# Adding x and three groups' projections on VectorE, and injecting the sums by two 64-column matmuls

## The chip, the cores and the metric

One Trainium2 chip, one core. The metric is the device time of one execution in microseconds. Every kernel was run several times. A run counts as slow when it is over 1.5% above the fastest of its kernel; those are left out of all comparisons. The profile is one traced execution; its span is mostly about 2.1 us shorter than the time, because the time includes start and end. In this kernel TensorE does the matmuls, whose sums gather in PSUM; VectorE and ScalarE do elementwise work and move sums out of PSUM (an eviction). An injection is a matmul with an identity that adds a finished row to the sums in PSUM.

## The reference, cut to what matters

One decode position goes through a cached attention block and an MLP block in parallel, and both are added to the input. Names that begin with `ln` are layer norms.

```python
x  = A_x                                   # (1, 1, 1024)
xn = ln(x)
# A: q = xn @ wq; 4 groups of 8 heads attend to 65536 cached keys each; o @ wo
# B: x1 = xn + shift(gelu(ln(xn) @ w1)) @ w2
#    out_B = x1 + gelu(ln(x1) @ w3) @ w4
out = x + A(xn) + B(xn)
# shift() moves quarters of the features by 1 or 2 positions and fills with zeros;
# with one position nothing is left of them, so its product with w2 is zero
```

The terms `x + xn` are an affine function of `x` (`x * ln_s1 + ln_s2` in the kernel). The output is thus that row, plus the projections of four groups of heads, plus the w4 product.

Of the kernel before, what the change touches and what calls it, by code (L numbers as in the profile page):

```python
# [8 lines left out]
BF16 = mybir.dt.bfloat16  # L9
F32 = mybir.dt.float32  # L10
ACTF = mybir.ActivationFunctionType
ALU = mybir.AluOpType
# [84 lines left out]
def kernel(  # L97
# [14 lines left out]
    nc = tc.nc  # L112
# [3 lines left out]
    D = A_x.shape[-1]  # L116
# [7 lines left out]
    FC = F // P  # L124
# [4 lines left out]
    NU = HKV * NB  # L129
# [3 lines left out]
    const = ctx.enter_context(tc.tile_pool(name="const", bufs=1))  # L133
    small = ctx.enter_context(tc.tile_pool(name="small", bufs=1))
    big = ctx.enter_context(tc.tile_pool(name="big", bufs=SLOTS))
    ppool = ctx.enter_context(tc.tile_pool(name="psb", bufs=1))
# [58 lines left out]
    st = Stream()  # L195

    x_row = ogpool.tile([32, D], BF16, name="x_row", tag="og")
# [4 lines left out]
    ident_f = const.tile([P, P], F32, name="ident_f")  # L202
# [9 lines left out]
    for b in range(2):  # L212
        nc.gpsimd.tensor_copy(
            out=spread[:, 2 * b:2 * b + 2, :].rearrange("p r (a i) -> p r a i", a=4),
            in_=ident_f[:, 64 * b:64 * b + 64].rearrange("p (i r) -> p r i", r=2).unsqueeze(2).to_broadcast([P, 2, 4, 32]))

    qdiag = const.tile([P, LEAD + 4 * P], BF16, name="qdiag")
    nc.gpsimd.memset(qdiag[:], 0.0)
    g_col = const.tile([P, 1], BF16, name="g_col")
    nc.gpsimd.memset(g_col[:], 0.0)  # L220

    psB = ps_B.tile([P, 512], F32, name="psB")

    def row_acc(j, lhsT, rhs, start=False):
        return nc.tensor.matmul(psB[32 * j:32 * j + 32, :], lhsT=lhsT.to_broadcast([lhsT.shape[0], 32]), rhs=rhs, start=start,  # L225
                                stop=False, tile_position=(0, 32 * j), skip_group_check=True)

    x_t = ppool.tile([P, DC, 32], BF16, name="x_t", tag="p")
    for a in range(4):
        nc.vector.transpose(out=x_t[32 * a:32 * a + 32].rearrange("p c j -> p (c j)"),  # L230
                            in_=x_row[:, 256 * a:256 * (a + 1)].rearrange("p (i c) -> p c i", c=DC))
# [3 lines left out]
    def layernorm(src, tag):  # L235
# [39 lines left out]
                          in_=sel8[:].unsqueeze(2).to_broadcast([P, 8, 16]))  # L275

    ln_s1 = const.tile([P, 1], F32, name="ln_s1")
    nc.vector.tensor_scalar(out=ln_s1[:], in0=rstd1[:], scalar1=1.0, scalar2=None, op0=ALU.add)
    ln_s2 = const.tile([P, 1], F32, name="ln_s2")
    nc.vector.tensor_tensor(out=ln_s2[:], in0=negmean1[:], in1=rstd1[:], op=ALU.mult)  # L280
    accx = ppool.tile([1, D], F32, name="accx", tag="p")
    nc.vector.tensor_scalar(out=accx[:], in0=x_row[0:1, :], scalar1=ln_s1[0:1, 0:1], scalar2=ln_s2[0:1, 0:1],
                            op0=ALU.mult, op1=ALU.add)
    for j in range(2):
        row_acc(j, ident_f[0:1, 0:1], accx[0:1, 512 * j:512 * (j + 1)], start=True)

    def row_matmul(acc, rep, cols, widths):
        for c in range(DC):
# [44 lines left out]
    def compute_w12():  # L333
        wt = st.tiles["w12"][:, 0:2 * DC * D].rearrange("p (w c n) -> p w c n", w=2, c=DC)
        ps1 = ps_S.tile([P, SUBS, 512], F32, name="ps1", tag="sc")
        for c in range(DC):
            for q in range(2):
                nc.tensor.matmul(ps1[0:32, q, :], lhsT=xn2_rep[:, c, :], rhs=wt[:, 0, c, 512 * q:512 * (q + 1)],
                                 start=(c == 0), stop=(c == DC - 1), tile_position=(0, 0))
        h1 = ppool.tile([32, 2, 512], BF16, name="h1", tag="p")  # L340
        nc.scalar.activation(out=h1[:], in_=ps1[0:32, 0:2, :], func=ACTF.Gelu_apprx_tanh)
        for c in range(DC):
            for j in range(2):
                row_acc(j, g_col[:], wt[:, 1, c, 512 * j:512 * (j + 1)])
        st.done("w12")

    group = {}
# [42 lines left out]
    def group_weights():  # L390
        nball = group["nball"]
        negmg = small.tile([P, 1], F32, name="negmg")
        nc.vector.tensor_reduce(out=negmg[:], in_=nball[:], axis=AX.X, op=ALU.min)
        wb = small.tile([P, NB], F32, name="wb")
        nc.scalar.activation(out=wb[:], in_=nball[:], func=ACTF.Exp, bias=negmg[:, 0:1], scale=-1.0)
        og = group["og"]
        nc.vector.tensor_scalar(out=og[:], in0=og[:], scalar1=wb[:, 0:1], scalar2=None, op0=ALU.mult)
        lw = small.tile([P, NB], F32, name="lw")
        ol = small.tile([P, DH + 1], F32, name="ol")
        nc.vector.tensor_tensor_reduce(out=lw[:], in0=group["lall"][:], in1=wb[:], scale=1.0, scalar=0.0,  # L400
                                       op0=ALU.mult, op1=ALU.add, accum_out=ol[:, DH:DH + 1])
        return og, wb, ol
# [3 lines left out]
    def compute_v(u):  # L406
        g, b = divmod(u, NB)
        if b == 1:
            og, wb, ol = group_weights()
        vt = st.tiles[("V", u)][:].rearrange("p (s u t d) -> p s u t d", u=SUBS, s=SETS, t=16)  # L410
        oacc = ps_O.tile([P, 512], F32, name="oacc")
        pT = group["p"]
        for e in range(SUBS):
            for t in range(16):
                q = t % 4
                mm = nc.tensor.matmul(oacc[32 * q:32 * (q + 1), :], lhsT=pT[:, e, 32 * t:32 * (t + 1)],  # L416
                                      rhs=vt[:, :, e, t, :], start=(e == 0 and t < 4),
                                      stop=(e == SUBS - 1 and t >= 12), tile_position=(0, 32 * q))
        st.done(("V", u))
        if b == 0:  # L420
            og = ogpool.tile([P, 512], F32, name="og", tag="og")
            nc.scalar.copy(out=og[:], in_=oacc[:])
            group["og"] = og
            return
        nc.vector.scalar_tensor_tensor(out=og[:], in0=oacc[:], scalar=wb[:, 1:2], in1=og[:],  # L425
                                       op0=ALU.mult, op1=ALU.add)
        group_rows(g, og, ol)
        return mm.ins

    oT = {}  # L430
    tail = {}
# [27 lines left out]
        return mm.ins if g == HKV - 1 else None  # L459

    def copy_projection():
        tail["o"] = st.tiles["w4"][0:1, FC * D:FC * D + 2 * D].bitcast(F32)
        nc.vector.tensor_copy(out=tail["o"].rearrange("p (j n) -> p j n", j=2), in_=tail["rows"][0:1, 0:2, :])  # L463

    def add_projection():
        for j in range(2):
            row_acc(j, ident_f[0:1, 0:1], tail["o"][:, 512 * j:512 * (j + 1)])

    def compute_w4(lo, hi):
        wt = st.tiles["w4"]  # L470
# [4 lines left out]
    compute_wq()  # L475
    compute_w3()
    compute_w12()
    for u in range(NU - 1):
        compute_k(u)
# [3 lines left out]
    for g in range(HKV - 1):  # L483
        project(g)
    copy_projection()
    summed = compute_v(NU - 1)
    with tc.issue_after(summed):
        add_projection()
    early = sum(W4_PIECES[:AT_ONCE])
    compute_w4(0, FIRST)  # L490
    with tc.issue_after(tail["gathered"]):
# [2 lines left out]
    with tc.issue_after(projected):  # L494
        compute_w4(early, FC - NARROW)
    sums = ogpool.tile([64, 512], F32, name="sums", tag="og")
    nc.scalar.copy(out=sums[:], in_=psB[0:64, :])
    quarters = [ps_M.tile([P, 512], F32, name="pm_r", tag="pm") for _ in range(2)]

    def quarter_acc(lhsT, rhs, start=False):  # L500
        for h in range(2):
            for j in range(2):
                q = 2 * h + j
                nc.tensor.matmul(quarters[h][32 * q:32 * q + 32, 0:256], lhsT=lhsT(j), rhs=rhs(j, h), start=start, stop=False,  # L504
                                 tile_position=(0, 32 * q), skip_group_check=True)

    def narrow_rows(lo, hi, start=False):
        wt = st.tiles["w4"]
        for c in range(lo, hi):
            quarter_acc(lambda j: hT[:, c:c + 1].to_broadcast([P, 32]),  # L510
                        lambda j, h: wt[:, D * c + 512 * j + 256 * h:D * c + 512 * j + 256 * (h + 1)],
                        start=start and c == lo)

    narrow_rows(FC - NARROW, FC - NARROW + AHEAD, start=True)
    quarter_acc(lambda j: ident_f[0:64, 32 * j:32 * j + 1].to_broadcast([64, 32]),
                lambda j, h: sums[:, 256 * h:256 * (h + 1)])
    narrow_rows(FC - NARROW + AHEAD, FC)

    out_t = ogpool.tile([64, 2, 256], BF16, name="out_t", tag="og")
# [3 lines left out]
                        in_=out_t[31:33].rearrange("p h n -> p (h n)"))  # L523
# [29 lines left out]
```

## The kernel before, the parts the change touches

All weights and the K and V caches pass once through three buffers of 128 x 32768 bf16, in a fixed order. A buffer's next load is issued when the last reader of its present content is done.

```python
stream = ["wq", "w3", "w12", K0, V0, K1, V1, ..., K7, "wo", V7, "w4"]   # each up to 8 MB
W4_PIECES = (8, 12, 5, 2, 1)      # w4's 28 chunks of 256 KB are loaded in five pieces
FIRST, AT_ONCE, NARROW, AHEAD = 3, 1, 8, 5
```

One PSUM tile, `psB`, collects the "first sums": rows 0 to 31 hold output columns 0 to 511, rows 32 to 63 hold columns 512 to 1023 (all 32 rows of a half are equal).

```python
def row_acc(j, lhsT, rhs, start=False):     # one 32-column matmul into half j
    return nc.tensor.matmul(psB[32*j:32*j+32, :], lhsT=lhsT.to_broadcast([lhsT.shape[0], 32]),
                            rhs=rhs, start=start, stop=False, tile_position=(0, 32*j), ...)

# at the start: x * ln_s1 + ln_s2 as one fp32 row, injected through a 1x1 identity
accx = ppool.tile([1, D], F32, name="accx", tag="p")
nc.vector.tensor_scalar(out=accx[:], in0=x_row[0:1, :], scalar1=ln_s1[0:1, 0:1], scalar2=ln_s2[0:1, 0:1], ...)
for j in range(2):
    row_acc(j, ident_f[0:1, 0:1], accx[0:1, 512*j:512*(j+1)], start=True)
...
# near the end: the first three groups' projections, summed in another PSUM tile ("o_acc")
def copy_projection():
    tail["o"] = st.tiles["w4"][0:1, FC*D:FC*D + 2*D].bitcast(F32)       # an unused corner of a buffer
    nc.vector.tensor_copy(out=tail["o"]..., in_=tail["rows"][0:1, 0:2, :])

def add_projection():
    for j in range(2):
        row_acc(j, ident_f[0:1, 0:1], tail["o"][:, 512*j:512*(j+1)])
...
for g in range(HKV - 1): project(g)          # 48 matmuls of one column
copy_projection()
summed = compute_v(NU - 1)                   # last V tile
with tc.issue_after(summed): add_projection()
compute_w4(0, FIRST)                         # w4 chunks 0..2
with tc.issue_after(tail["gathered"]): compute_w4(FIRST, early)    # 3..7
projected = project(HKV - 1)                 # last group, into psB
with tc.issue_after(projected): compute_w4(early, FC - NARROW)     # 8..19
sums = ogpool.tile([64, 512], F32, name="sums", tag="og")
nc.scalar.copy(out=sums[:], in_=psB[0:64, :])
quarters = [...]                             # two PSUM tiles: the output in four quarters of 256
narrow_rows(FC - NARROW, FC - NARROW + AHEAD, start=True)          # chunks 20..24, four matmuls each
quarter_acc(lambda j: ident_f[0:64, 32*j:32*j+1].to_broadcast([64, 32]),
            lambda j, h: sums[:, 256*h:256*(h+1)])                 # inject the first sums
narrow_rows(FC - NARROW + AHEAD, FC)         # chunks 25, 26 (fourth piece), 27 (fifth piece)
# cast the quarters (half on ScalarE, half on VectorE), store
```

## Time and profile before

| | before |
|---|---|
| time, median of the first 3 runs | 400.86 us (400.77 to 400.88) |
| span of the traced execution | 398.7 us |
| TensorE / VectorE / ScalarE busy | 58% / 53% / 7% |
| big DMA queue, share of 16 engines' time | 98.9% |
| loaded | 169.87 MB, 426 GB/s over the span |

The page of the kernel before. The line of busy times gives us, share of the span and the number of instructions of each engine; the queue line gives packets, MB and share of 16 engines' span.

```profile
span 398.7 us, 2595 instructions
...
PE 229.6 (58%) x1372; PEld 44.2 (11%) x878; DVE 209.4 (53%) x155; ACT 27.6 (7%) x36; POOL 5.3 (1%) x28
...
q1 hardware_dynamic: 4128, 169.87, 98.9%
...
HBM read 169.87 MB, written 0.00 MB: 426 GB/s over the span
```

No compute engine is near its limit, and the load queue is. The Trainium skill, "DMA: Bandwidth & Descriptors", section Measured, gives 425 GB/s for a 16 MB transfer that GpSimd issued; the 426 GB/s of this trace, whose loads SyncE issues, agree with it. So the whole of the span is filled with loads at about the rate that one may expect.

The end of the chain of waits of the kernel before (start us, us, what): what ended last, followed back.

```profile
340.47 17.43 DVE big L361 x4
...
357.94 3.64 PE sc L366 x16
...
363.39 33.10 DMA big<-in_B_w_dram
...
396.54 0.34 PE pm_r L504 x4
...
396.90 0.43 DVE out_t L521
```

The last K tile is transposed and multiplied, then its buffer is free, the five pieces of w4 are issued into it, and 33.10 us later the last of them has landed. The pieces are issued behind loads that are still under way, so these 33 us are a place in the stream, not the cost of w4 alone.

Timeline of the kernel before (start us, us, engine, line, operation, tiles, count; in brackets the idle time of the engine just before and what ended it). First the end of the x injection (the second of its two groups) and wq's matmuls, then the end:

```profile
19.07 1.91 PE L225 MATMUL psB<-accx,ident_f 1*32 1x512 f32 x2
...
21.92 5.02 PE L291 MATMUL psq<-big,ln_rep_a 128*32 128x512 bf16 x64 [0.94 <-DMA big<-in_A_wq_dram]
```
```profile
380.70 1.21 DVE L463 COPY big<-o_acc 1x1024 f32<-1x1024 f32 x1 [10.50 <-PE o_acc L456]
...
384.05 1.05 PE L225 MATMUL psB<-big,ident_f 1*32 1x512 f32 x4
...
386.76 0.49 PE L438 MATMUL pm_e<-ol,sel8big 128*128 128x129 f32 x2 [0.92 <-DVE ol L437]
...
391.54 2.77 PE L225 MATMUL psB<-big,hT 128*32 128x512 bf16 x24 [1.31 <-DMA big<-in_B_w_dram]
...
394.34 0.58 ACT L497 COPY sums<-psB 64x512 f32<-64x512 f32 x1 [26.75 <-PE psB L225]
...
394.65 0.73 PE L504 MATMUL pm_r<-big,hT 128*32 128x256 bf16 x20 [0.34 <-DMA big<-in_B_w_dram]
...
395.31 0.64 PE L504 MATMUL pm_r<-sums,ident_f 64*32 64x256 f32 x8
...
395.90 0.40 PE L504 MATMUL pm_r<-big,hT 128*32 128x256 bf16 x8
396.54 0.29 PE L504 MATMUL pm_r<-big,hT 128*32 128x256 bf16 x4 [0.24 <-DMA big<-in_B_w_dram]
```

Read the idle times. TensorE waits 0.94 us for wq at the start, 1.31 and 0.34 us for w4's second and third pieces near the end, and 0.24 us for the last piece just before the end. Each of these is a cushion: work placed ahead of it can shrink, or grow by about that much, without moving what follows. An fp32 matmul stands in the trace as two records (x8 for four injections).

### The profile page before, as it was taken

The page shows a single profiled execution, that of the slowest core. Times are in us where ns is not written, and L with a number is a line of the kernel's source. Part 1 is how long each engine was busy: PE and PEld are TensorE (multiplying, and loading weights), DVE is VectorE, ACT ScalarE, POOL GpSimd, SP SyncE. Part 2 cuts the span into 40 slices and gives each one's busy share as a digit, 9 for nine tenths or more (in the row PEclk, how much of TensorE's full clock was granted, in tenths as well). Part 3 has the DMA queues.
Part 4 walks back from the last instruction along what each step waited for, and adds up shares of the span by engine and source line. Part 5 has one row for each costly group of instructions (what it writes and reads, how often), then busy time and mean ns, then how long its engine had stood idle before and what let it go on. Part 6 is the DMA issues. An engine that isn't in the chain of part 4 may idle for free.

```text
span 398.7 us, 2595 instructions
## 1 busy us (share of the span) xinstructions
PE 229.6 (58%) x1372; PEld 44.2 (11%) x878; DVE 209.4 (53%) x155; ACT 27.6 (7%) x36; POOL 5.3 (1%) x28
## 2 busy tenths in 40 slices
PE   0461960591569238733974296519462955394996
PEld 0210000010100010011001010200020101010132
DVE  0620010974296559633963795269439942894140
ACT  1001010003000200020002000200110001002000
POOL 2000000000000000000000000000000000000000
PEclk9995996596869787966695889679956896698799
DMA  9998999999999999999999999999999998999996
GB/s 421 421 443 377 444 434 487 441 421 421 416 422 434 421 480 442 421 421 427 422 434 427 447 460 427 416 427 427 441 429 427 454 441 385 418 460 429 409 432 254
DMA packets 4144, 170.03 MB, mean 427 GB/s; under 512 B 419, under 2 KB 421, under 8 KB 678
## 3 DMA queue, kind: packets, MB, share of 16 engines
q1 hardware_dynamic: 4128, 169.87, 98.9%
q8 instruction: 9, 0.15, 0.2%
q14 instruction: 1, 0.01, 0.0%
q10 hardware_dynamic: 6, 0.00, 0.0%
HBM read 169.87 MB, written 0.00 MB: 426 GB/s over the span
## 4 chain that ended last, share of the span: by engine, by line
DMA 56%; DVE 21%; PE 17%; ACT 2%; another core or an unknown queue 2%; issue 1%; SPq 0%; DVEq 0%; ACTq 0%
DMA big<-in_A_k_cache_dram 42%; DVE big L361 15%; PE sc L366 11%; DMA big<-in_B_w_dram 8%; DMA big<-in_A_wq_dram 5%; PE oacc L416 4%; DVE p_sb L387 2%; DVE mx L371 2%; ACT p_sb L384 2%; PE psq L291 1%; SPq L187 0%; PE pm_mx L373 0%; DVE m L375 0%; PE pm_mx L380 0%
## 5 line engine op out<-in xcount | busy, mean ns | idle before, releaser
L366 PE MATMUL sc<-big,qdiag 128*128 128x512 bf16 x512 | 129.3, 414 | 67.0 <-DVE big L361 61.4
L361 DVE STREAM_TRANSPOSE big<-big 128x4096 f32<-128x4096 f32 x32 | 139.4, 4413 | 50.3 <-DMA big<-in_A_k_cache_dram 50.3
L416 PE MATMUL oacc<-big,p_sb 128*32 128x512 bf16 x512 | 43.0, 502 | 34.5 <-DVE p_sb L387 34.5
L371 DVE TENSOR_REDUCE mx<-sc 128x1 f32<-128x2048 f32 x8 | 18.3, 2292 | 29.8 <-PE sc L366 29.8
L366 PEld LDWEIGHTS <-qdiag 128*128 128x128 bf16 x128 | 13.2, 103 | 178.7 <-issue 145.9
L384 ACT ACTIVATE p_sb<-sc,nball 128x2048 bf16<-128x2048 f32 x8 | 15.7, 1967 | 220.9 <-DVE nball L382 220.9
L387 DVE STREAM_TRANSPOSE p_sb<-p_sb 128x2048 bf16<-128x2048 bf16 x8 | 18.5, 2311 | 18.0 <-ACT p_sb L384 18.0
L416 PEld LDWEIGHTS <-p_sb 128*32 128x32 bf16 x512 | 16.1, 122 | 58.2 <-DVE p_sb L387 35.1
L291 PE MATMUL psh<-big,ln_rep_b 128*32 128x512 bf16 (+1 forms) x64 | 12.4, 943 | 8.8 <-DMA big<-in_B_w_dram 8.8
L456 PE MATMUL o_acc<-big,oT 128*1 128x512 bf16 x48 | 13.2, 445 | 2.4 <-ACT p_sb L384 2.4
L373 PE MATMUL pm_mx<-ident_f,mx 128*1 128x128 f32 x8 | 2.4, 296 | 19.1 <-DVE mx L371 19.1
L425 DVE SCALAR_TENSOR_TENSOR og<-oacc,wb,og 128x512 f32<-128x512 f32 x4 | 3.0, 751 | 18.4 <-PE oacc L416 18.4
L330 DVE STREAM_TRANSPOSE h_row<-h_row 128x896 bf16<-128x896 bf16 x1 | 1.1, 1111 | 22.0 <-ACT h_row L329 22.0
L239 PE MATMUL pm_ln<-ln_rowsum_a,ones_f 128*128 128x1 f32 x2 | 0.6, 348 | 12.8 <-DVE ln_rowsum_a L237 12.8
L438 PE MATMUL pm_e<-ol,sel8big 128*128 128x129 f32 x8 | 2.3, 370 | 8.8 <-DVE ol L437 8.8
L315 POOL COPY qdiag<-qx 32x32 bf16<-32x32 bf16 x16 | 3.2, 202 | 279.3 <-PE sc L366 250.9
L230 DVE STREAM_TRANSPOSE x_t<-x_row 32x256 bf16<-32x256 bf16 x4 | 2.5, 616 | 8.3 <-DMA x_row<-in_A_x_dram 8.3
L463 DVE COPY big<-o_acc 1x1024 f32<-1x1024 f32 x1 | 1.2, 1211 | 10.5 <-PE o_acc L456 10.5
L225 PE MATMUL psB<-big,hT 128*32 128x512 bf16 x40 | 4.8, 380 | 1.3 <-DMA big<-in_B_w_dram 1.3
L291 PE MATMUL psq<-big,ln_rep_a 128*32 128x512 bf16 x64 | 5.0, 482 | 0.9 <-DMA big<-in_A_wq_dram 0.9
L521 DVE CAST out_t<-pm_r 64x256 bf16<-64x256 f32 x1 | 0.4, 426 | 8.6 <-PE pm_r L504 8.6
L380 PE MATMUL pm_mx<-ident_f,rep 1*128 1x1 f32 x8 | 1.8, 229 | 5.0 <-DVE rep L377 5.0
(101 smaller groups left out, 76.2 us busy)
## 6 DMA issues: line engine op xcount, KB each, us to landing
big<-in_A_wo_dram SPq DMA_DIRECT2D x1, 8192.0 KB, 35.8
big<-in_B_w_dram SPq DMA_DIRECT2D x1, 7168.0 KB, 38.0
big<-in_B_w_dram SPq DMA_DIRECT2D x3, 2048.0 KB, 35.5
big<-in_B_w_dram SPq DMA_DIRECT2D x1, 3072.0 KB, 29.5
big<-in_B_w_dram SPq DMA_DIRECT2D x1, 1280.0 KB, 32.2
big<-in_B_w_dram SPq DMA_DIRECT2D x1, 512.0 KB
big<-in_B_w_dram SPq DMA_DIRECT2D x1, 256.0 KB, 33.1
big<-in_A_k_cache_dram SPq DMA_DIRECT2D x8, 42.3
```

The costliest lines, as they stand in the source:

```text
L225: return nc.tensor.matmul(psB[32 * j:32 * j + 32, :], lhsT=lhsT.to_broadcast([lhsT.shape[0], 32]), rhs=rhs, start=start, stop=False, tile_ ...
L230: nc.vector.transpose(out=x_t[32 * a:32 * a + 32].rearrange("p c j -> p (c j)"), in_=x_row[:, 256 * a:256 * (a + 1)].rearrange("p (i c) -> ...
L291: nc.tensor.matmul(acc[32 * q:32 * q + 32, i, 0:n], lhsT=rep[:, c, :], rhs=cols(c, i, q), start=(c == 0), stop=(c == DC - 1), tile_positio ...
L315: nc.gpsimd.tensor_copy(out=qdiag[at, LEAD:].rearrange("p (x c) -> p x c", x=4)[:, :, 32 * a:32 * a + 8], in_=qx[at, :, 8 * g:8 * g + 8])
L361: nc.vector.transpose(out=words, in_=words)
L366: nc.tensor.matmul(sc[:, e, :], lhsT=qdiag[:, c0:c0 + P], rhs=cols[:, s, e, :, b2, :, r], start=(s == 0 and b2 == 0 and r == 0), stop=(s = ...
L371: nc.vector.reduce_max(out=mx[:], in_=sc[:].rearrange("p e n -> p (e n)"), axis=AX.X)
L384: nc.scalar.activation(out=p_sb[:], in_=sc[:], func=ACTF.Exp, bias=nball[:, b:b + 1], scale=SCALE, accum_out=group["lall"][:, b:b + 1])
L387: nc.vector.transpose(out=flat, in_=flat)
L416: mm = nc.tensor.matmul(oacc[32 * q:32 * (q + 1), :], lhsT=pT[:, e, 32 * t:32 * (t + 1)], rhs=vt[:, :, e, t, :], start=(e == 0 and t < 4), ...
L425: nc.vector.scalar_tensor_tensor(out=og[:], in0=oacc[:], scalar=wb[:, 1:2], in1=og[:], op0=ALU.mult, op1=ALU.add)
L456: nc.tensor.matmul(tail["rows"][0:1, h2, :], lhsT=oT[g][:, j:j + 1], rhs=wt[:, g, j, 512 * h2:512 * (h2 + 1)], start=(g == 0 and j == 0), ...
```

## The change

The intent is to take the fp32 injections off TensorE. The row x is now kept as two halves on partitions 0 and 32. Near the end VectorE forms `x * ln_s1 + ln_s2`, adds the three groups' projections from PSUM, and adds the result to the first sums as it moves them out of PSUM. The final injection is done by two 64-column matmuls in place of four 32-column ones.

```diff
+    x_halves = const.tile([64, 512], BF16, name="x_halves")
+    nc.gpsimd.memset(x_halves[:], 0.0)
...
-    accx = ppool.tile([1, D], F32, name="accx", tag="p")
-    nc.vector.tensor_scalar(out=accx[:], in0=x_row[0:1, :], ...)
     for j in range(2):
-        row_acc(j, ident_f[0:1, 0:1], accx[0:1, 512 * j:512 * (j + 1)], start=True)
+        nc.vector.tensor_copy(out=x_halves[32 * j:32 * j + 1, :], in_=x_row[0:1, 512 * j:512 * (j + 1)])
...                                             # the first w2 row now starts the accumulation
     def copy_projection():
-        tail["o"] = st.tiles["w4"][0:1, FC * D:FC * D + 2 * D].bitcast(F32)
-        nc.vector.tensor_copy(out=tail["o"]..., in_=tail["rows"][0:1, 0:2, :])
-    def add_projection():
+        tail["o"] = st.tiles["w4"][0:64, FC * D:FC * D + D].bitcast(F32)
+        nc.vector.tensor_scalar(out=tail["o"], in0=x_halves[:], scalar1=ln_s1[0:64, 0:1], scalar2=ln_s2[0:64, 0:1], ...)
         for j in range(2):
-            row_acc(j, ident_f[0:1, 0:1], tail["o"][:, 512 * j:512 * (j + 1)])
+            row = tail["o"][32 * j:32 * j + 1, :]
+            nc.vector.tensor_tensor(out=row, in0=tail["rows"][0:1, j, :], in1=row, op=ALU.add)
...
-    summed = compute_v(NU - 1)
-    with tc.issue_after(summed):
-        add_projection()
+    compute_v(NU - 1)
...
-    nc.scalar.copy(out=sums[:], in_=psB[0:64, :])
+    nc.vector.tensor_tensor(out=sums[:], in0=psB[0:64, :], in1=tail["o"], op=ALU.add)
...
-    quarter_acc(lambda j: ident_f[0:64, 32 * j:32 * j + 1].to_broadcast([64, 32]),
-                lambda j, h: sums[:, 256 * h:256 * (h + 1)])
+    pick = small.tile([64, 2, 32], F32, name="pick", tag="msk")        # two identity columns, 32 times each
+    nc.vector.tensor_copy(out=pick[:], in_=ident_f[0:64, 0:64]....to_broadcast([64, 2, 32]))
+    for h in range(2):
+        nc.tensor.matmul(quarters[h][64 * h:64 * h + 64, 0:256], lhsT=pick[:]..., rhs=sums[:, 256 * h:256 * (h + 1)],
+                         tile_position=(0, 64 * h), ...)
```

More of the change, by code (lines that the diff above doesn't have):

```diff
@@ L280 @@
     nc.vector.tensor_tensor(out=ln_s2[:], in0=negmean1[:], in1=rstd1[:], op=ALU.mult)
-    accx = ppool.tile([1, D], F32, name="accx", tag="p")
-    nc.vector.tensor_scalar(out=accx[:], in0=x_row[0:1, :], scalar1=ln_s1[0:1, 0:1], scalar2=ln_s2[0:1, 0:1],
-                            op0=ALU.mult, op1=ALU.add)
     for j in range(2):
-        row_acc(j, ident_f[0:1, 0:1], accx[0:1, 512 * j:512 * (j + 1)], start=True)
+        nc.vector.tensor_copy(out=x_halves[32 * j:32 * j + 1, :], in_=x_row[0:1, 512 * j:512 * (j + 1)])
     def row_matmul(acc, rep, cols, widths):
@@ L343, in compute_w12 @@
             for j in range(2):
-                row_acc(j, g_col[:], wt[:, 1, c, 512 * j:512 * (j + 1)])
+                row_acc(j, g_col[:], wt[:, 1, c, 512 * j:512 * (j + 1)], start=(c == 0))
         st.done("w12")
@@ L461, in copy_projection @@
     def copy_projection():
-        tail["o"] = st.tiles["w4"][0:1, FC * D:FC * D + 2 * D].bitcast(F32)
-        nc.vector.tensor_copy(out=tail["o"].rearrange("p (j n) -> p j n", j=2), in_=tail["rows"][0:1, 0:2, :])
-    def add_projection():
+        tail["o"] = st.tiles["w4"][0:64, FC * D:FC * D + D].bitcast(F32)
+        nc.vector.tensor_scalar(out=tail["o"], in0=x_halves[:], scalar1=ln_s1[0:64, 0:1], scalar2=ln_s2[0:64, 0:1],
+                                op0=ALU.mult, op1=ALU.add)
         for j in range(2):
-            row_acc(j, ident_f[0:1, 0:1], tail["o"][:, 512 * j:512 * (j + 1)])
+            row = tail["o"][32 * j:32 * j + 1, :]
+            nc.vector.tensor_tensor(out=row, in0=tail["rows"][0:1, j, :], in1=row, op=ALU.add)
     def compute_w4(lo, hi):
@@ L514 @@
     narrow_rows(FC - NARROW, FC - NARROW + AHEAD, start=True)
-    quarter_acc(lambda j: ident_f[0:64, 32 * j:32 * j + 1].to_broadcast([64, 32]),
-                lambda j, h: sums[:, 256 * h:256 * (h + 1)])
+    pick = small.tile([64, 2, 32], F32, name="pick", tag="msk")
+    nc.vector.tensor_copy(out=pick[:],
+                          in_=ident_f[0:64, 0:64].rearrange("p (j r) -> p j r", r=32)[:, :, 0:1].to_broadcast([64, 2, 32]))
+    for h in range(2):
+        nc.tensor.matmul(quarters[h][64 * h:64 * h + 64, 0:256], lhsT=pick[:].rearrange("p j r -> p (j r)"), rhs=sums[:, 256 * h:256 * (h + 1)], start=False,
+                         stop=False, tile_position=(0, 64 * h), skip_group_check=True)
     narrow_rows(FC - NARROW + AHEAD, FC)
```

## The prediction

> **What bounds the kernel now.** The loads. The queue table gives the big DMA queue 98.9% of 16 engines' time; 169.87 MB at 426 GB/s is the span, 398.7 us. TensorE is 58% busy, VectorE 53%. The chain of waits ends: last K tile landed (340.4 us), VectorE transposes 17.4 us, score matmuls 3.6 us, then (361.6 us) its buffer is free and w4's five pieces are issued; 33.1 us of DMA; last four matmuls at 396.54 us (0.34 us); cast 0.43 us; store. That chain contains neither the x injection, nor the projected rows, nor the eviction of the first sums.
>
> **What the change does, durations from the timeline.**
> 1. Start: two fp32 injections leave TensorE (1.88 and 1.91 us, between 16.75 and 21 us) and a 0.79 us VectorE operation. Added: a POOL memset, two small copies. TensorE waits for wq until 21.92 us (0.94 us idle, ended by DMA). Worth 0.
> 2. Last K tile: a 64x512 tensor_scalar enters VectorE between the maximum (ends 363.89) and the reduce that waits for TensorE until 364.26. Estimated 0.45 us (the 128x512 scale): softmax 0.1 to 0.2 us later.
> 3. The 1.21 us copy of the projected rows (380.70) becomes two 1x512 additions, estimated 1.3 to 1.5 us together; VectorE's next work waits for V until 384.18. Worth 0.
> 4. Two injections after V (4 records, 1.05 us at 384.05) go. The gather matmul waits for VectorE until 386.76, later the w4 matmuls for DMA until 391.54 (1.31 us idle). That idle swallows this and point 2's delay.
> 5. The sums' eviction moves from ScalarE (0.58 us at 394.34) to VectorE as an addition, estimated 0.6 to 0.75 us from 128x512 operations at 0.69 to 0.75. Ready near 395.05, before the narrow matmuls ahead end (395.38). Hidden. The selector's copy runs earlier in an idle VectorE.
> 6. Four 32-column fp32 injections (8 records, 0.64 us) become two of 64 columns (4 records, about 0.32 us). This is next to the end, but after it the last four matmuls still waited 0.24 us for w4's last piece. That wait becomes about 0.5 us.
>
> **On the critical path:** about 0; perhaps 0.1 to 0.3 us in executions where the last piece lands earlier. No load, its order, or release of a buffer changes.
>
> **Predicted time:** 400.75 us, range 400.1 to 401.4 (the runs before lie within 0.11 us; I leave room for another chip and small shifts of the loads). Faster by over 2%: 0.01. Within 2%: 0.98. Slower by over 2%: 0.01.
>
> **What would show each step.** Right: queue share about 99%, 426 GB/s; the chain of waits ends as above, through about 33 us of DMA; idle before the last four narrow matmuls grows from 0.24 to about 0.5 us, ended by DMA; the addition of the sums takes 0.6 to 0.75 us; the injection is 4 records in about 0.32 us; the first wq matmul is still released by wq's landing. Wrong: the injection waits for VectorE; the chain passes through the sums, the projected rows or TensorE instead of DMA; w4's issue moves from 361.6 us.
>
> **What would make it wrong.** With a longer TensorE pause after V (about 384.9 to 386.8 us) its clock may drop; the Trainium skill, "TensorE: Matmul & The Clock Gate", What's actually happening, puts that at an idle window of about 3.4 us, more than this pause; the trace's 1.31 us pause slowed nothing. If it did drop, the 2.77 us of w4 sums would stretch and the tail grow by a microsecond. Or the loads pace differently by tenths for reasons outside the program.

## The result, and the profile after

The changed kernel took 400.83 us (median of 6 runs, 400.73 to 401.06), the kernel before 400.88 us (6 runs, 400.77 to 401.12). The ratio is 0.9998 with a 95% interval of 0.9986 to 1.0011: no difference. Ratios here and below are the mean time of one kernel's fast runs over that of the other's of the same rounds, so not quite the ratio of the medians that are quoted.

The page and the end of the chain of waits after:

```profile
span 398.6 us, 2575 instructions
...
PE 225.4 (57%) x1360; PEld 44.0 (11%) x866; DVE 210.7 (53%) x160; ACT 27.1 (7%) x35; POOL 5.8 (1%) x29
...
q1 hardware_dynamic: 4128, 169.87, 98.9%
```
```profile
340.39 17.43 DVE big L360 x4
...
357.87 3.65 PE sc L365 x16
...
363.32 33.11 DMA big<-in_B_w_dram
...
396.48 0.34 PE pm_r L501 x4
...
396.84 0.43 DVE out_t L522
```

TensorE is busy 4.2 us less (229.6 to 225.4). The queue's share is 98.9% as before, and the chain has the same links with the same lengths: 33.11 us of DMA where it was 33.10. The traced end is 0.06 us earlier, but so was the start of the transposes of the last K tile (340.39 against 340.47), before anything at the end had been touched. That much is drift of the loads.

The timeline after: the start, the last K tile, and the end.

```profile
21.99 4.98 PE L290 MATMUL psq<-big,ln_rep_a 128*32 128x512 bf16 x64 [3.73 <-DMA big<-in_A_wq_dram]
```
```profile
363.75 0.53 DVE L462 TENSOR_SCALAR big<-x_halves,ln_s,ln_s 64x512 f32<-64x512 bf16 x1
...
363.88 0.27 PE L372 MATMUL pm_mx<-ident_f,mx 128*1 128x128 f32 x1 [2.38 <-DVE mx L370]
364.20 0.27 DVE L374 TENSOR_REDUCE m<-pm_mx 1x8 f32<-1x128 f32 x1
```
```profile
380.45 1.39 DVE L466 TENSOR_TENSOR big<-o_acc,big 1x512 f32<-1x512 f32 x2 [10.31 <-PE o_acc L455]
...
386.73 0.49 PE L437 MATMUL pm_e<-ol,sel8big 128*128 128x129 f32 x2 [1.74 <-DVE ol L436]
...
391.49 2.77 PE L227 MATMUL psB<-big,hT 128*32 128x512 bf16 x24 [1.30 <-DMA big<-in_B_w_dram]
...
394.29 0.68 DVE L494 TENSOR_TENSOR sums<-psB,big 64x512 f32<-64x512 f32 x1 [5.97 <-PE psB L227]
...
395.25 0.65 PE L516 MATMUL pm_r<-sums,pick 64*64 64x256 f32 x4
...
395.83 0.40 PE L501 MATMUL pm_r<-big,hT 128*32 128x256 bf16 x8
396.48 0.29 PE L501 MATMUL pm_r<-big,hT 128*32 128x256 bf16 x4 [0.24 <-DMA big<-in_B_w_dram]
```

Every saving shows up as idle time. TensorE's idle before wq grew from 0.94 to 3.73 us; before the gather matmul it grew from 0.92 to 1.74 us. The waits for w4's second and last pieces did not change (1.30 and 0.24 us).

One line contradicts the prediction. The last injection has half the records (x4, not x8) and takes just as long: 0.65 us against 0.64, and 0.58 us from its start to the next row's start (395.25 to 395.83), against 0.59 before. The experiments begin there.

### The profile page after: what moved, and what is told of

It is laid out like the page before. It is cut to its first block, busy times and chain, and to the rows that moved or that the text cites. A ratio compares the mean times of both kernels' runs of the same rounds, so it can differ in the third digit from the quotient of the medians.

```text
span 398.6 us, 2575 instructions
## 1 busy us (share of the span) xinstructions
PE 225.4 (57%) x1360; PEld 44.0 (11%) x866; DVE 210.7 (53%) x160; ACT 27.1 (7%) x35; POOL 5.8 (1%) x29
## 3 DMA queue, kind: packets, MB, share of 16 engines
q1 hardware_dynamic: 4128, 169.87, 98.9%
## 4 chain that ended last, share of the span: by engine, by line
DMA 56%; DVE 21%; PE 17%; ACT 2%; another core or an unknown queue 2%; issue 1%; SPq 0%; DVEq 0%; ACTq 0%
DMA big<-in_A_k_cache_dram 42%; DVE big L360 15%; PE sc L365 11%; DMA big<-in_B_w_dram 8%; DMA big<-in_A_wq_dram 6%; PE oacc L415 4%; DVE p_sb L386 2%; DVE mx L370 2%; ACT p_sb L383 2%; PE psq L290 1%; SPq L187 0%; PE pm_mx L372 0%; DVE m L374 0%; PE pm_mx L379 0%
## 5 line engine op out<-in xcount | busy, mean ns | idle before, releaser
L466 DVE TENSOR_TENSOR big<-o_acc,big 1x512 f32<-1x512 f32 x2 | 1.4, 679 | 10.3 <-PE o_acc L455 10.3
```

## The experiments

Theory A: the stream of loads decides the time, and everything that the change removes lies in cushions. Rivals: B, the 64-column injection really is cheaper by half and something hides it; C, TensorE paces the end; D, the removed fp32 injections were on the path and another cost has cancelled them. The experiments first settle the last injection, then put back multiples of the removed work to find out how large the cushions are, and then change the loads.

### One step undone: four narrow injections in the changed kernel

```diff
-    pick = ...                                           # and its copy on VectorE
-    for h in range(2): nc.tensor.matmul(..., lhsT=pick ..., tile_position=(0, 64 * h))
+    quarter_acc(lambda j: ident_f[0:64, 32 * j:32 * j + 1].to_broadcast([64, 32]),
+                lambda j, h: sums[:, 256 * h:256 * (h + 1)])
```

> The changed kernel with only its last step undone: four 32-column injections again in place of two of 64 columns. Theory A (loads decide; the four narrow injections ran side by side, so their cost is the time in which one streams, 0.58 us from the first injection to the first row after it, for both forms): the same spacing of 0.58 us within 0.05, idle of 0.24 us before the last four narrow matmuls, ratio to before within 0.1%. Rival B (the 64-column form is cheaper by half as predicted, something else has hidden it): spacing about 0.9 us in this kernel, and the time 0.1 to 0.3 us longer than that of the changed kernel.

Four fast runs had 400.80 to 401.09 us against a median of 400.80 us for the kernel before, ratio 1.0004 (0.9990 to 1.0018). The profile fell in an execution at a granted clock of 0.625 and a time of 422.86 us, so its spacings are not compared with anything. The time fits A, but does not exclude B, whose 0.1 to 0.3 us lie inside the interval. The next three runs decide.

### The last injection two and four times

The selector (or identity) is divided by the number of repetitions, so the results stay right.

```diff
-    nc.vector.tensor_copy(out=pick[:], in_=...)
+    nc.vector.tensor_scalar(out=pick[:], in0=..., scalar1=1.0 / n, scalar2=None, op0=ALU.mult)   # n = 2 or 4
-    for h in range(2): nc.tensor.matmul(...)
+    for _ in range(n):
+        for h in range(2): nc.tensor.matmul(...)
```

> The changed kernel with the selector halved and its pair of injections done twice (same result). Theory A: the last rows of the second w4 piece start 0.58 us later; the wait of 0.24 us for the last load swallows part; plus 0.15 to 0.40 us against before, the idle before the last four narrow matmuls gone or near 0. If TensorE already paced the end (rival C), plus 0.58 us. If the end had much more room than the profile shows, plus 0.

> The selector at a quarter, the pair of injections done four times (same result). Theory A: three times 0.58 us more TensorE work minus the same cushion: plus 1.3 to 1.6 us against before, and 1.16 us more than the doubled kernel. Rival C (no cushion): plus 1.74 us.

> Four 32-column injections done four times, each with a quarter of the value (same result). Theory A (both forms cost the same): equal to the 64-column kernel done four times within 0.15 us. Rival B (the 64-column form costs about half): at least 1.0 us longer than it.

| | median us | minus before (400.80) | ratio (95%) |
|---|---|---|---|
| 64 columns, twice | 400.99 | +0.19 | 1.0006 (0.9993 to 1.0018) |
| 64 columns, four times | 401.78 | +0.98 | 1.0024 (1.0010 to 1.0037) |
| 32 columns, four times | 401.86 | +1.06 | 1.0026 (1.0013 to 1.0038) |

The injection and the rows behind it, in the timelines of the three kernels in that order:

```profile
395.29 1.08 PE L518 MATMUL pm_r<-sums,pick 64*64 64x256 f32 x8
...
396.30 0.53 PE L501 MATMUL pm_r<-big,hT 128*32 128x256 bf16 x12
```
```profile
397.04 1.94 PE L518 MATMUL pm_r<-sums,pick 64*64 64x256 f32 x16 [0.23 <-DVE sums L494]
...
398.91 0.51 PE L501 MATMUL pm_r<-big,hT 128*32 128x256 bf16 x12
```
```profile
395.21 1.93 PE L501 MATMUL pm_r<-sums,ident_q 64*32 64x256 f32 x32
...
397.07 0.51 PE L501 MATMUL pm_r<-big,hT 128*32 128x256 bf16 x12
```

From the first injection to the first row it takes 1.01 us for two repetitions and 1.87 us for four in the wide form, so 0.43 us for each more ((1.87 - 1.01) / 2); the traced execution of the latter is its slowest, but its granted clock was 1.00 in this stretch (397 to 398.9 us). The narrow form takes 1.86 us for four; with the 0.59 us for one in the kernel before, that is 0.42 us for each more. The two forms cost the same, and B falls. There are twice as many narrow matmuls, but they stand on different column groups of the array and run side by side; what takes the time is streaming 256 fp32 columns once.

The size fits as well. The Trainium skill, "FP8 and Floating Point Precision", section TensorE Precision Notes, says that true fp32 needs four passes through the array, and "TensorE: Matmul & The Clock Gate", section What's actually happening, gives 2.4 GHz for the full clock. An estimate from both is 4 x 256 / 2.4 GHz = 0.427 us, and the runs show 0.42 to 0.43. The remaining 0.15 us of a single injection's 0.58 is paid once, however often it is repeated.

These runs also show the cushion at the end. A second injection adds 0.43 us of TensorE work. The median rose by 0.19 us, but its interval (-0.28 to +0.72 us) is too wide to say how much was swallowed. The traced execution says it better. In the first fence above, all 12 rows follow each other without a wait. Four rows of this kind take 0.11 us more of TensorE ((0.73 - 0.40) / 3, from the groups of 20 and of 8 in the kernel before), so the last four began near 396.52 us. Before they began at 396.54 us, and in the changed kernel at 396.48. Nearly all of the 0.43 us was swallowed, and not only the idle time of 0.24 us. That idle time is counted from the modelled end of the eight rows, 0.40 us after their start; the last four could have begun 0.22 us after it. The room was thus about 0.43 us (396.48 - 395.83 - 0.22): an idle time after short matmuls can understate a cushion.

Three more injections add 1.29 us of work and 0.98 or 1.06 us of time. My expectation of 1.3 to 1.6 us was too high because it charged 0.58 us for each repetition. Rival C expected the whole of the added work. At the measured pace that is 1.29 us, which the intervals (up to about +1.5 us) do not exclude. The traces do: in the narrow kernel the last four rows began near 397.29 us (397.07 + 0.22), 0.75 us later than before, for 1.27 us of added work; and with one more injection they hardly moved.

### No last injection at all

```diff
-    pick = ...                                           # and its copy on VectorE
-    for h in range(2):
-        nc.tensor.matmul(quarters[h]..., lhsT=pick ..., rhs=sums ...)
```

> The changed kernel without its last injection (a wrong result on purpose: the first sums are missing from the output). Theory A: the idle before the last four narrow matmuls grows from 0.24 us to about 0.8 us, and the time stays within 0.1% of before: even a free injection gains nothing. Rival C (TensorE paces the end): minus 0.3 to 0.6 us.

The result is wrong as meant. The time was 400.82 us against 400.71, ratio 1.0006 (0.9993 to 1.0018): even a free injection gains nothing, as A says. But the wait did not appear where A had put it.

```profile
391.72 2.77 PE L227 MATMUL psB<-big,hT 128*32 128x512 bf16 x24 [1.41 <-DMA big<-in_B_w_dram]
...
396.07 0.40 PE L501 MATMUL pm_r<-big,hT 128*32 128x256 bf16 x8 [0.53 <-DMA big<-in_B_w_dram]
...
396.71 0.29 PE L501 MATMUL pm_r<-big,hT 128*32 128x256 bf16 x4 [0.24 <-DMA big<-in_B_w_dram]
```

The 0.24 us before the last four rows stayed at 0.24. A new wait of 0.53 us stands before the eight rows of the fourth piece. This execution ran 0.23 us later than the changed kernel's (391.72 against 391.49), so these rows start at 395.84 on the changed kernel's clock, where they started at 395.83 with the injection. The fourth piece therefore lands just as the injection ends. There are two cushions in a row at the end, and a shorter injection is taken up by the first of them.

### The x injection at the start, four times

```diff
+    part = const.tile([1, 1], F32, name="part")          # 1/4
-    for j in range(2): row_acc(j, ident_f[0:1, 0:1], accx..., start=True)
+    for i in range(4):
+        for j in range(2): row_acc(j, part[:], accx..., start=i == 0)
```

> The kernel before with the x injection at the start done four times, each with a quarter of the value (same result): some 11 us more fp32 work on TensorE before the first wq matmul. Theory A (the loads are queued so far ahead that the start has room): the first wq matmuls start about 10 us later (near 32 us, not 21.92), and the time stays within 0.1% of before. Rival D (TensorE's work at the start is paid, so that removing it should have gained): plus 3 us or more.

Measured 400.63 us (400.59 to 400.66) against 400.86, ratio 0.9990 (0.9977 to 1.0003).

```profile
25.89 5.60 PE L294 MATMUL psq<-big,ln_rep_a 128*32 128x512 bf16 x64
```

The first wq matmul started at 25.89 us, 4 us later than before, and not at 32 us: three more repetitions cost 1.66 us each ((25.89 - 20.91) / 3, 20.91 us being where the first weights for wq were loaded before), not the 3.8 us that I had summed from two groups' durations. Still, wq had landed 4 us before TensorE came to it, and the time did not rise. Rival D falls for the start: the loads behind wq are queued already. Even these 1.66 us are slow: the trace has a new pair of weight loads every 0.85 us here, against 0.43 us after V in the next section. TensorE thus ran at half that pace from about 17 to 30 us, though the profile prints a granted clock of 1.00 there. The trace has no clock record before 29.93 us (24.76 us in the kernel before), so that 1.00 says nothing.

### The projected rows' injection after V, four and eight times

```diff
     def add_projection():
-        for j in range(2): row_acc(j, ident_f[0:1, 0:1], tail["o"]...)
+        for _ in range(n):                               # n = 4 or 8, each with 1/n
+            for j in range(2): row_acc(j, part[:], tail["o"]...)
```

> The kernel before with the injection of the projected rows after V done four times, each with a quarter (same result): about 2.6 us more TensorE work at 384 us. Theory A (idle time after V swallows it): the gather matmul and the wo rows about 1.3 to 1.7 us later, the 1.31 us wait for w4's second-to-last large piece nearly gone, the time plus 0 to 0.3 us. Rival D (this work is on the path): plus 2.6 us.

> The same eight times with an eighth each: about 6.0 us more TensorE work after V. Theory A: minus an idle of about 0.9 us before the gather matmul, 1.3 us before the w4 sums and some tenths before the end: plus 3.0 to 3.8 us, with the DMA wait before the w4 sums gone. Rival D: plus 6 us.

Both cost more than A expected. Four times: 402.63 us against 400.86 with a wide spread (401.46 to 405.75 in six runs), ratio 1.0058 (1.0026 to 1.0089). Eight times: 408.58 us (408.35 to 412.10), plus 7.7 us, ratio 1.0208. Rival D's numbers (2.6 and 6 us) don't fit either: the larger dose costs more than the added work at the pace that I had counted. The trace says why. Timeline of the eightfold kernel, and the table of engine busy time by stretch (busy us and count for TensorE, its weight loads, VectorE, ScalarE, POOL; then granted clock, DMA share, GB/s):

```profile
386.23 8.84 PE L225 MATMUL psB<-big,part 1*32 1x512 f32 x22
...
395.00 3.43 PE L225 MATMUL psB<-big,hT 128*32 128x512 bf16 x16
...
398.26 1.89 PE L225 MATMUL psB<-big,oT 128*32 128x512 bf16 x16
```
```profile
388.00:395.00 7.00, 7.00 (x16) 1.28 (x13) 0.00 (x0) 0.00 (x0) 0.00 (x0) 0.50 0.92 385
395.00:398.20 3.20, 3.20 (x17) 1.18 (x18) 0.00 (x0) 0.00 (x0) 0.00 (x0) 0.51 0.12 44
398.20:402.00 3.80, 3.80 (x40) 1.72 (x38) 0.00 (x0) 0.00 (x0) 0.00 (x0) 1.00 0.02 4
```

The granted clock fell from 1.00 (0.94 from 387 to 388 us) to 0.50 at about 388 us, although TensorE was busy without a pause (5.00 of 5.00 us from 383 to 388, and 7.00 of 7.00 us after). The injections stretched, and the sixteen bf16 matmuls behind them took 3.43 us where the next sixteen took 1.89. Only about 10 us later was the clock whole again. The traced fourfold execution (405.75 us, its slowest run) has the same: clock 0.50 from 387 to 391 us. So in these two executions a series of single-row fp32 matmuls did not hold the clock. The two that the kernel before had did not cost it: its clock is 1.00 from 380 to 395 us in the trace.

What follows for the change: the two injections themselves were inside the cushion (before and after have the same time), but the cushion that I had worked out from idle times alone is no guide to larger doses, because the added work changes the speed of what follows. How much of the fourfold kernel's spread is the clock is shown for one execution only and stays open for the others.

### Moving the sums in two steps

```diff
-    nc.vector.tensor_tensor(out=sums[:], in0=psB[0:64, :], in1=tail["o"], op=ALU.add)
+    nc.scalar.copy(out=sums[:], in_=psB[0:64, :])
+    nc.vector.tensor_tensor(out=sums[:], in0=sums[:], in1=tail["o"], op=ALU.add)
```

> The changed kernel with the sums first copied by ScalarE and then added to by VectorE (same result): the sums are ready about 0.6 us later, near 395.5 us. Theory A: the injection then waits for VectorE about 0.3 to 0.4 us, and part of this is swallowed by the 0.24 us wait for the last load: plus 0 to 0.25 us. A rival by which the eviction is on the path: plus 0.6 us.

Measured 401.19 us against 400.86, ratio 1.0011 (0.9994 to 1.0028). The six runs fall apart: four have spans of 398.6 to 398.8 us like the kernel before, two have 400.4 and 400.6. The median lies above A's range (plus 0.33 us against 0 to 0.25), because of these two and because the traced execution took 401.55 us at a span of 398.7, where its span does not explain the excess. In this traced one the injection waited 0.34 us for VectorE, as expected, and the end did not move: the cushion swallowed it. A rival that puts the eviction on the path expected 0.6 us in all runs. The two longer executions have no trace. A traced execution of the fourfold 64-column kernel, at 403.44 us where its other four runs have 401.64 to 401.80, shows what such a one can look like:

```profile
391.81 4.02 PE L227 MATMUL psB<-big,hT 128*32 128x512 bf16 x20 [2.00 <-DMA big<-in_B_w_dram]
```
```profile
391.80:395.40 3.60, 3.59 (x18) 1.58 (x19) 0.00 (x0) 0.00 (x0) 0.00 (x0) 0.53 0.81 328
```

Here TensorE had paused for 2.00 us before w4's second piece, the clock came back at about half, and 20 of the 24 sums took 4.02 us where all 24 take 2.77. This is the drop of the clock that the prediction named as its risk, though after another pause, seen in one execution. It is not the change's alone to show: two other kernels without the injection after V had pauses of 2.45 us there at full clock (the twofold 64-column and the fourfold 32-column one), and the kernel before also has a few executions with a span longer by 0.9 us (3 of its first 35 runs), untraced; and one of its 11 runs in the last round took 405.36 us, at a mean granted clock of 0.683 against 0.80 to 0.82 in the others. Whether the change makes such executions more or less frequent is open; in its own six runs there was none.

### Fewer bytes, late, early, and more of them

```diff
# late: four of the eight chunks of w4's first piece, neither loaded nor multiplied
+                    k = 4 if c0 == 0 else n                # the load takes k chunks in place of n
-    compute_w4(FIRST, early)
+    compute_w4(FIRST, 4)
# early: half of w1, neither loaded nor multiplied
-    go(out=t[:, 0:DC * D], in_=B_w1...)          # and its loop over DC chunks
+    go(out=t[:, 0:4 * D], in_=B_w1...[:, 0:4, :]...)   # and a loop over 4
```

> The changed kernel without four of the eight chunks of w4's first piece, neither loaded nor multiplied (a wrong result on purpose): 1.05 MB less, estimated 2.46 us at 427 GB/s, at the end of the stream. Theory A: the last load lands some 2.4 us earlier, but the chain through V and the wo rows, which has 1.3 us of room there, then decides: minus 1.2 to 2.0 us. If loads were not what decides: 0.

> The changed kernel with half of w1 neither loaded nor multiplied (the result stays right, because what w1 feeds is multiplied by zeros in this shape): the same 1.05 MB less, early in the stream. Theory A (the stream of loads paces everything): every later landing is 2.46 us earlier, and so is the end: minus 2.2 to 2.6 us. Rival (a chain of computation and buffer releases after the start decides): clearly less, below 1 us.

The late cut gave 398.90 us against 400.71 (minus 1.81, ratio 0.9952), the early cut 398.48 (minus 2.23, ratio 0.9949). Both are 1.05 MB, about 2.46 us at 427 GB/s. The early cut's chain of waits is the old one, with the w4 loads' wait 2.28 us earlier (361.04 against 363.32 us) and as long as before:

```profile
361.04 33.09 DMA big<-in_B_w_dram
```

The late cut was capped: without the wait for w4, its chain runs through V, the gather and the wo rows, with no DMA after V. In the kernel before, the waits for loads on that chain are 1.31, 0.34 and 0.24 us, together 1.89 us, so it could not yield all 2.46 us. The comparison called the late cut's result correct although four chunks of w4 were missing; its tolerance does not notice them, so this pass says nothing. The passes of the two runs with less of w1 and w2 say little too; there the argument is that the code multiplies w2 by zeros.

The cuts point to a faster version. For one position the product with w2 is zero whatever w1 and w2 hold (as long as they are finite), and the kernel multiplies w2 by a column of zeros. The last run leaves both out:

```diff
-    stream = ["wq", "w3", "w12"]
+    stream = ["wq", "w3"]
-    compute_w12()
     def compute_w4(lo, hi): ...
-                row_acc(j, hT[:, c:c + 1], wt[...])
+                row_acc(j, hT[:, c:c + 1], wt[...], start=c == 0)
```

> The changed kernel without w1 and w2, neither loaded nor multiplied; the w4 sums start the accumulation (the result stays right for one position, where what they feed is shifted out and multiplied by zeros). 4.19 MB less, four times the early cut of 1.05 MB, which gave 2.2 us; estimated 9.8 us at 427 GB/s. Theory A (the stream of loads paces everything): minus 9.0 to 10.0 us. Rival (a chain of computation and buffer releases decides in the middle): minus 6 us or less, with a lower share of the DMA queue (below 98%).

390.81 us (390.67 to 390.93, 6 runs) against 400.72: minus 9.91 us, ratio 0.9742 (0.9706 to 0.9778, with the 405.36 us of before in it), result correct. The span and the queue line of its page:

```profile
span 389.1 us, 2527 instructions
...
q1 hardware_dynamic: 3840, 165.68, 98.8%
```

Four times the bytes of the early cut gave 4.4 times the gain, the queue is as full as ever (98.8%), and the wait of 0.23 us before the last rows is still there. It is the fastest kernel, about 2.5% below both; it holds only for one position, which the kernel asserts anyway.

## Why the prediction was right

It was right in the time (400.75 us said, 400.83 us measured, range 400.1 to 401.4) and in the reason: 4.2 us of TensorE work went, no load moved, and every saving became idle time ended by a load or by VectorE. The runs on fewer bytes show that the loads decide; those that repeat the injections show that at the start and at the end there is room. Point by point:

1. Start, worth 0: right. The idle before wq grew to 3.73 us, and four times the old work there did not lengthen the run.
2. Softmax later by 0.1 to 0.2 us: it was not. The operation took 0.53 us and ended at 364.28, but the reduce behind it started at 364.20, 0.05 us after TensorE's transpose of the maxima had ended (363.88 + 0.27). Before, those were 364.26 and 0.04. The two overlap where I had added one to the other.
3. Two additions of 1.3 to 1.5 us: 1.39 us, hidden.
4. Idle after V swallows the removed injections: right. The gather matmul started at 386.73, still released by VectorE.
5. Eviction and addition 0.6 to 0.75 us: 0.68 us, ready at 394.97, hidden.
6. "Four 32-column fp32 injections (8 records, 0.64 us) become two of 64 columns (4 records, about 0.32 us)": wrong. It took 0.65 us. The step counted records, as though they ran one after the other; they run side by side, and one repetition costs 0.42 us as four narrow matmuls and 0.43 us as two wide ones. "That wait becomes about 0.5 us" failed with it, and would have failed anyway: without any injection the new wait stands before the fourth piece's rows, and the last one stays at 0.24 us.

The wrong step cost nothing in time because it sat in front of a wait for a load. In a kernel whose end is paced by TensorE it would have promised 0.3 us that do not exist.

## What to carry to other kernels

When loads fill the span, look for the waits that end in a load and ask what stands before each: a saving there only lengthens the wait. Count matmuls that stand on different column groups by the time that one of them streams, not by their number; merging them into a wider one saved instructions here, not time. And before trusting an idle stretch as room for more work, look at the granted clock after it: behind the added fp32 matmuls with one row it was half.

## What the Trainium skill lacked or had wrong

- "TensorE: Matmul & The Clock Gate", section What's actually happening, ties the clock to how busy TensorE is. For matmuls other than transposes it lacks that some may not hold the clock: behind fp32 matmuls of one row and 32 columns the granted clock fell to 0.50 at 388 us of the eightfold kernel, with TensorE busy 5.00 of 5.00 us before and 7.00 of 7.00 us after. At the start of the kernel with the x injection four times, TensorE was busy 8.00 of 8.00 us (18 to 26 us), mostly with such matmuls, at half the pace that they had after V; the pace doubled only 4 us after wq's matmuls began. bf16 matmuls of 128 rows and one column, in the kernel before, brought it from 0.50 (367.5 to 372.5 us) back to full. Rows and type differ both, so which of them matters is open.
- The same section puts the fall of the clock at an idle window of about 3.4 us. One execution lost the clock after a pause of 2.00 us; two others kept it through 2.45 us. A pause shorter than the window can be enough. One thing that differs is where the pause falls: the changes in the traces' clock records lie whole multiples of 3.41 us apart, and by them the 2.00 us lay inside one such stretch, while an edge cut each pause of 2.45 us into about 1.6 and 0.8 us. That alone does not decide it: a pause of 1.97 us inside one stretch (the sums moved in two steps) kept the clock.
- The same page, Part 3 on packing, tells what overlaps but gives no number for fp32. Here one more repetition of four 32-column fp32 matmuls of 256 columns cost 0.42 us, and of two 64-column ones 0.43 us, which agrees with four passes of one stream.
